# Shifted V by GpSimd, mixer factors by SyncE, one pair a load, relu engine by place, no zero products: one change to an attention and mixer kernel

## The chip, the cores and the metric

The kernel runs on one core of one Trainium2 chip. The metric is device time in microseconds (us). The engines are PE (TensorE), DVE (VectorE), ACT (ScalarE), POOL (GpSimd) and SP (SyncE, which here only issues DMAs). Profiles are single executions, and the hardware profiler's span is about 2 us shorter than the time of the same run.

A run is called slow when it is more than 1.5% above the fastest run of the same kernel. Ratios below are the mean time of one kernel's fast runs over that of the other's fast runs of the same rounds, so they are not quite the ratios of the medians that are quoted beside them.

## The reference

```python
# q, k, v: (4, 8, 768, 64); window of 96 keys behind the query, and 8 global keys
scores = q @ k^T / 8 - slope[h] * dist      # -1e9 outside window and globals
x = softmax(scores) @ v                     # to (4, 768, 512)
u = x + ((x^T @ U) @ V)^T                   # low-rank mixing of tokens, rank 32
out = u + relu(u @ w_ch1) @ w_ch2           # w_ch1 (512, 2048), w_ch2 (2048, 512)
```

## The kernel before

The work is cut into 16 slots, one per pair of heads (4 batches of 4 pairs). Slot i computes scores of pair i+1, A.V of pair i, the mixing of pair i, and prepares q, k, v of pair i+2. The MLP of a batch can start only when its four pairs are done, so slots 0 to 3 have no MLP work for PE. From slot 4 on, MLP pieces of the earlier batch are filled in between (`fill`), each of four 512-column matmuls. After slot 15 comes a tail of MLP work only.

A query block needs the keys and values of its own block and of the block before it, where the first rows are replaced by those of block 0 (the global keys). For the values this is the tile `vp`:

```python
def v_prev(i):
    vh = v16[:, i % VR]; vp = vp16[:, i % VPR]
    if i == 0:
        nc.vector.tensor_copy(vp, vh[:, :, 0:NPB])
        nc.vector.tensor_copy(vp[0:G], vh[0:G, :, 0:1].broadcast_to(...))
    else:                                        # SBUF to SBUF, three DMAs
        nc.sync.dma_start(vp[G:P], vh[G:P, :, 0:NPB])
        for hi in range(2):
            nc.sync.dma_start(vp[0:G, hi], vh[0:G, hi, 0:1].broadcast_to(...))

def keep_busy(n):                                # products of zeros
    if KEEP and n:
        bank = ps_tp("dmy", FP32, 512)
        for _ in range(n):
            nc.tensor.matmul(bank, zz[:, 0:P], zz, start=True, stop=True)

# in a piece of the first MLP product
if jt % 2 == 0: nc.scalar.activation(htr[:, jt], hh, AF.Relu)
else:           nc.vector.tensor_scalar_max(htr[:, jt], hh, 0.0)

keep_busy(15)
# ... (cut)
for i in range(NPAIR):                           # slots 0 to 3
    v_prev(i + 2)
    if i > 0: mix_h(i - 1, nc.vector)
    scores(i + 1, 0); transposes(i + 2, 0); scores(i + 1, 1)
    keep_busy(2); av(i); norm(i)
    scores(i + 1, 2); cast_x(i); mask(i + 1, 0); transposes(i + 2, 1)
    keep_busy(3); k_prev(i + 2, nc.gpsimd)
    if i > 0: mix_t(i - 1)
    mask(i + 1, 1); keep_busy(3); mix_tmp(i)
    if i == 0: load(4, 2)
    if i == 1: load_w2()
    if i == 2: load(6, 2)
mix_h(NPAIR - 1, nc.vector); keep_busy(6); mix_t(NPAIR - 1)
```

All loads that convert to half precision (q, k, v, w1, w2, and here also the mixer's U and V) are issued by GpSimd, in program order with its copies `k_prev`.

The softmax here doesn't subtract the row's maximum and nothing guards it: scores larger than these inputs give would overflow.

## Time and profile before

Time: 269.16 us median (268.44 to 269.26, 4 runs). The profiled span is 265.7 us.

| mark in the profile | before, us |
|---|---|
| A.V of pair 0 starts | 16.7 |
| A.V of pair 1 starts, ends | 24.0, 31.6 |
| first MLP matmul (`hps`, slot 4) | 53.4 |
| A.V of pair 8 starts | 98.2 |
| from there to the end of the span | 167.5 |

First, the profile's second part: the span in 40 slices of 6.6 us, busy tenths of PE, the granted PE clock, and the DMA engines.

```profile
PE   8785498868989999899999999989998999999994
...
PEclk9979579999999999999999999999999999999999
DMA  7999999999999999915991162413215101210022
```

The DMA engines are busy at 9 tenths or more from the second slice to the seventeenth, up to about 110 us. The clock dips in the third and in the fifth and sixth slice.

PE's waits (engine, line, what it waited for: us in total, times, longest):

```profile
PE ob L335 <- DMA vp_85<-v_84: 5.9, 2, 3.6
PE hps L428 <- ACT htr L433: 3.2, 5, 0.7
PE sc L297 <- POOL kP L260: 2.1, 1, 2.1
...
PE hps L428 <- DVE htr L435: 1.1, 1, 1.1
```

The largest is the wait for `vp`. Its origin is in the chain of waits that ended last (start us, us, what):

```profile
14.08 0.70 SPq L272
14.82 0.62 SPq L274
15.48 15.33 DMA vp_85<-v_84
30.85 0.22 PE ob L335
```

The last of pair 1's three copies, a small one of 20 KB, was issued at 15.48 us and landed at 30.8, while the 2 MB of w1, issued at 11.3 and 12.0 us, were under way (they landed at 25.9 and 31.3). Late in this run, at 158 us, the same small copy landed in 2.0 us. That w1 is what held it is inferred from these times. The Trainium skill, "Trainium Kernel Development and Optimization", Key Constraints, says that DMAs issued from SyncE, ScalarE and GpSimd run on the same 16 DMA engines and interleave. The trace is in keeping with it: the large `vp` copies, issued by SyncE, take 2.4 us to land at best in this run, and 12.2 us at worst, beside loads that GpSimd had issued.

### The profile page before, as it was taken

The page shows a single profiled execution, that of the slowest core. Times are in us where ns is not written, and L with a number is a line of the kernel's source. Part 1 is how long each engine was busy: PE and PEld are TensorE (multiplying, and loading weights), DVE is VectorE, ACT ScalarE, POOL GpSimd, SP SyncE. Part 2 cuts the span into 40 slices and gives each one's busy share as a digit, 9 for nine tenths or more (in the row PEclk, how much of TensorE's full clock was granted, in tenths as well). Part 3 has the DMA queues.
Part 4 walks back from the last instruction along what each step waited for, and adds up shares of the span by engine and source line. Part 5 has one row for each costly group of instructions (what it writes and reads, how often), then busy time and mean ns, then how long its engine had stood idle before and what let it go on. Part 6 is the DMA issues. An engine that isn't in the chain of part 4 may idle for free.

```text
span 265.7 us, 4667 instructions
## 1 busy us (share of the span) xinstructions
PE 239.0 (90%) x1910; PEld 116.0 (44%) x1910; DVE 133.7 (50%) x225; ACT 99.7 (38%) x180; POOL 69.5 (26%) x98
## 2 busy tenths in 40 slices
PE   8785498868989999899999999989998999999994
PEld 3352355434544553344444454445453444444441
DVE  3644257737566575624544645576666342234321
ACT  1786167445724525322246141557411330023100
POOL 8905035568248184104801010101000000000000
PEclk9979579999999999999999999999999999999999
DMA  7999999999999999915991162413215101210022
GB/s 82 165 194 214 201 157 176 183 157 152 156 148 144 231 109 152 107 32 163 162 183 27 30 123 83 123 38 79 35 69 80 39 0 42 79 39 0 2 79 79
DMA packets 97958, 28.67 MB, mean 108 GB/s; under 512 B 86225, under 2 KB 94353, under 8 KB 97937
## 3 DMA queue, kind: packets, MB, share of 16 engines
q0 software_dynamic: 62736, 13.73, 58.4%
q1 hardware_dynamic: 35200, 14.64, 27.4%
q8 instruction: 15, 0.25, 0.4%
q14 instruction: 7, 0.05, 0.1%
HBM read 27.46 MB, written 6.29 MB: 127 GB/s over the span
## 4 chain that ended last, share of the span: by engine, by line
PE 61%; DMA 16%; ACT 7%; POOL 5%; DVE 5%; issue 3%; SPq 1%; DVEq 0%; POOLq 0%; ACTq 0%
PE cps L446 27%; PE hps L428 23%; DMA vp_85<-v_84 6%; DMA v_84<-in_v_dram 5%; ACT ep L302 4%; PE sc L297 4%; DMA qkT<-qkn 4%; POOL qkn L121 2%; DVE x_sb L388 2%; DMA v16w<-in_moe_V_dram 2%; PE h_ps L383 1%; PE ob L335 1%; POOL v_84 L110 1%; PE ob L339 1%; PE tmp_ps L369 1%
## 5 line engine op out<-in xcount | busy, mean ns | idle before, releaser
L428 PE MATMUL hps<-uT,w_16_81 128*128 128x512 f16 x384 | 91.4, 379 | 5.5 <-ACT htr L433 3.2
L446 PE MATMUL cps<-w_16_82,htr 128*128 128x512 f16 x384 | 88.6, 379 | 0.0
L302 ACT ACTIVATE ep<-sc 128x512 f16<-128x512 f32 (+1 forms) x96 | 48.6, 564 | 71.0 <-PE sc L297 71.0
L428 PEld LDWEIGHTS <-w_16_81 128*128 128x128 f16 x384 | 35.1, 97 | 48.1 <-issue 11.4
L433 ACT ACTIVATE htr<-hps 128x512 f16<-128x512 f32 x48 | 28.7, 598 | 65.1 <-PE hps L428 64.5
L446 PEld LDWEIGHTS <-htr 128*128 128x128 f16 x384 | 35.5, 98 | 40.2
L435 DVE TENSOR_SCALAR htr<-hps 128x512 f16<-128x512 f32 x48 | 33.1, 689 | 36.6 <-PE hps L428 36.6
L453 DVE TENSOR_TENSOR osb<-cps,x_sb 128x512 f32<-128x512 f32 x24 | 16.5, 689 | 30.7 <-PE cps L446 30.6
L315 DVE TENSOR_TENSOR ep<-ep,expb 128x1280 f16<-128x1280 f16 x32 | 26.5, 828 | 9.5 <-ACT ep L302 9.4
L259 POOL COPY kP<-qkT 128x480 f16<-128x480 f16 x10 | 6.5, 654 | 79.9 <-DMA qkT<-qkn 68.8
L388 DVE TENSOR_TENSOR x_sb<-x_sb,h_ps 128x768 f32<-128x768 f32 x16 | 15.3, 953 | 14.1 <-PE h_ps L383 14.1
L207 PE MATMUL dmy<-zz 128*128 128x512 f16 x60 | 19.6, 454 | 1.3 <-DVE zz L149 1.2
L121 POOL DMA_DIRECT2D qkn<-in_k_dram x20 | 16.8, 851 | 8.3 <-DMA v_84<-in_v_dram 4.7
L335 PE MATMUL ob<-vp_85,ep 128*128 128x65 f16 x160 | 13.5, 199 | 5.9 <-DMA vp_85<-v_84 5.9
L351 DVE RECIPROCAL rcp<-ob 128x12 f32<-128x12 f32 x16 | 3.7, 233 | 28.5 <-PE ob L339 28.5
L121 POOL DMA_DIRECT2D qkn<-in_q_dram x20 | 16.7, 852 | 0.0
L352 DVE TENSOR_TENSOR x_sb<-ob,rcp 128x768 f32<-128x768 f32 x16 | 15.3, 958 | 0.6
L335 PEld LDWEIGHTS <-ep 128*128 128x128 f16 x160 | 11.8, 102 | 5.9 <-DMA vp_85<-v_84 4.0
L339 PE MATMUL ob<-v_84,ep 128*128 128x65 f16 x160 | 13.5, 199 | 0.0
L339 PEld LDWEIGHTS <-ep 128*128 128x128 f16 x160 | 11.7, 101 | 2.4 <-issue 2.4
L110 POOL DMA_DIRECT2D v_84<-in_v_dram x9 | 12.1, 1346 | 0.2
L392 DVE CAST uu<-x_sb 128x768 f16<-128x768 f32 x16 | 9.6, 600 | 0.6
(120 smaller groups left out, 157.4 us busy)
## 6 DMA issues: line engine op xcount, KB each, us to landing
out_dram<-osb SPq DMA_DIRECT2D x24, 256.0 KB, 2.2
v_84<-in_v_dram POOLq DMA_DIRECT2D x7, 384.0 KB, 8.4
w_16_81<-in_moe_w_ch_dram POOLq DMA_DIRECT2D x2, 1024.0 KB, 17.0
w_16_82<-in_moe_w_ch_dram POOLq DMA_DIRECT2D x2, 1024.0 KB, 14.5
qkn<-in_q_dram POOLq DMA_DIRECT2D x20, 96.0 KB, 7.3
qkn<-in_k_dram POOLq DMA_DIRECT2D x20, 96.0 KB, 6.7
vp_85<-v_84 SPq DMA_DIRECT2D x15, 121.9 KB, 6.5
qkst<-in_q_dram POOLq DMA_DIRECT2D x2, 384.0 KB, 9.5
```

Source lines behind the costliest of these rows:

```text
L121: nc.gpsimd.dma_start(stg[:, :, hi], src[b, 2 * hp + hi].rearrange("(n p) d -> p n d", p=P),)
L207: nc.tensor.matmul(bank, zz[:, 0:P], zz, start=True, stop=True)
L302: nc.scalar.activation(ep[:, hi, idx[0]:idx[0] + n].rearrange("p n c -> p (n c)"), scs[hi][:, 0:n * P], AF.Exp, scale=qk_scale,)
L315: nc.vector.tensor_tensor(blk, blk, eb[:, :, m:m + 1].broadcast_to((P, 2, NPB, P)), ALU.mult,)
L335: nc.tensor.matmul(ob[:, t], ep[:, hi, NSB + t - 1], vp16[:, i % VPR, hi, t - 1], start=True, stop=False,)
L339: nc.tensor.matmul(ob[:, t], ep[:, hi, t - 1], v16[:, i % VR, hi, t], start=False, stop=True,)
L388: nc.vector.tensor_tensor(xp, xp, hps[:, 0:S].rearrange("p (n c) -> p n c", n=NSB), ALU.add)
L428: nc.tensor.matmul(hh, w1_16[:, dc, jt * P:(jt + 1) * P], uT[:, dc, r0:r0 + TT], start=(dc == 0), stop=(dc == NDC - 1),)
L433: nc.scalar.activation(htr[:, jt], hh, AF.Relu)
L435: nc.vector.tensor_scalar_max(htr[:, jt], hh, 0.0)
L446: nc.tensor.matmul(cps, htr[:, jc, tt * P:(tt + 1) * P], w2_16[:, jc], start=(jc == 0), stop=(jc == NJC - 1),)
L453: nc.vector.tensor_tensor(osb, cps, xs[b][:, n], ALU.add)
```

## The change

Five ideas: make the shifted V of pairs 1 to 5 with GpSimd copies, so it does not queue behind weight loads; load the mixer factors U and V by SyncE and convert them on ScalarE, to free GpSimd's issue time; load one pair a slot; give each MLP piece's relu to the engine that has room at that place; and leave out the products of zeros. Some steps of slots 0 to 3 also change places.

```diff
-    KEEP = True
+    KEEP = False
...
+    u32 = uv32[:, S:S + NSB * R].rearrange("p (c r) -> p c r", c=NSB)
+    nc.sync.dma_start(u32, moe_U.rearrange("(c p) r -> p c r", p=P))
+    for g in range(NGR):
+        nc.sync.dma_start(uv32[g * R:(g + 1) * R, 0:S], moe_V)
+    nc.scalar.activation(u16, u32, AF.Copy)
+    nc.scalar.activation(v16w, uv32[:, 0:S], AF.Copy)
-    nc.gpsimd.dma_start(u16, ...)          # and v16w by GpSimd, copied by SyncE
...
-        if i == 0:
-            nc.vector.tensor_copy(vp, vh[:, :, 0:NPB])
-            nc.vector.tensor_copy(vp[0:G], ...)
+        if i < NSTART:                     # NSTART is 6
+            eng = nc.vector if i == 0 else nc.gpsimd
+            eng.tensor_copy(vp, vh[:, :, 0:NPB])
+            eng.tensor_copy(vp[0:G], ...)
...
-                if jt % 2 == 0:
+                if on_act:                 # set at each fill(f, True or False), alternating within it
...
     for i in range(NPAIR):
-        v_prev(i + 2)
...                                         # transposes(2, 0) after av(0)
-        keep_busy(2)
+        keep_busy(1)
...
         k_prev(i + 2, nc.gpsimd)
+        v_prev(i + 2)
+        mix_tmp(i)
+        mask(i + 1, 1)
         if i > 0:
             mix_t(i - 1)
-        mask(i + 1, 1)
-        keep_busy(3)
-        mix_tmp(i)
...
-        if i == 2:
-            load(6, 2)
+        if i >= 2:
+            load(i + 4, 1)
...
-        if i % 2 == 0 and i + 4 < NP:
-            load(i + 4, 2)
+        if i + 4 < NP:
+            load(i + 4, 1)
```

## The prediction

> **What bounds it now.** From 53.4 us on (first hps matmul in the timeline) TensorE is nearly full: the windows 80 to 200 us show PE 92 to 99% busy, and its waits after 53 us sum to 10 us (2.1 for kP, 4.3 for relu, 1.2 for osb and uT; wait view). 768 matmuls of 512 columns at 216 ns (64 in 13.83 us in the chain) are 166 us of it. Before 53.4 us nothing is full. In this startup pair 1's products with vp wait 3.65 + 2.26 us for SyncE's shift of V: its three DMAs, issued at 14.1 to 15.5 us, land at 24.2, 27.8 and 30.8, behind the 2 MB of w1. Half clock is granted at 15.5 to 18.9 and 25.7 to 36.0 us. A.V of pairs 0 to 3 starts at 16.7, 24.0 (done at 31.4), 39.1, 46.0. An undisturbed slot is 6.8 us: a chain av, norm (1.2), cast (0.84), mix_tmp, tmp16, mix_h, add (0.96), beside 5.5 to 6.4 us of ScalarE.
>
> **What the change does.**
> 1. Pairs 1 to 5: 15 DMA issues become 10 GpSimd copies. By kP's copies (480 elements 0.6 us, 160 in 0.32) I estimate 1.5 to 2 us a pair on POOL, which has room (2.8 and 3.8 us busy in 10 to 20 and 20 to 30 us). Removes the 5.9 us wait and its slow restart: estimate 7 us.
> 2. U and V by SyncE plus two ScalarE copies (estimate 1.1 us): frees 1.4 us of POOL issue, so pairs 2, 3 and w1 start earlier; adds DMA load beside the first q, k. Net -1 to +0.5 us.
> 3. 60 zero matmuls go: 19.6 us busy, mostly in PE's idle time. The 15 at the start hold the first transposes until 6.5 us although q landed at 4.7; in a slot two groups sit on the chain, 0.4 us each. Against it: the Trainium skill, "TensorE: Matmul & The Clock Gate", Part 1, says that the array defaults to half clock until about 3.4 us of sustained work; the half clock around this trace's idle stretch agrees. I expect much of the startup at 0.5: av 1.3 instead of 0.7 us, a slot about 7.5 us rather than 6; recovered in the first 4 us of MLP work.
> 4. mix_tmp before the second mask: tmp16 0.7 us earlier a slot. One pair per load: kP of pair 5 no longer sits behind eight qkn issues, so the 2.1 us wait goes; but DMA stays the limit for pairs 4 and 6 (q4 landed 34.3, k6 58.7), so part of the gain is waited for again.
> 5. Relu engine by place: of 4.3 us of waits for htr, about 2 go.
>
> **Sum.** MLP starts at about 46 instead of 53.4 us (-7); its stage has 1 us for restarting cold and up to 2 of new waits for qkT, against 2 (kP) and 2 (relu) gained: -1 to -3. Predicted 259.5 us, range 254 to 265.5. Chances: faster 0.84, same 0.14, slower 0.02.
>
> **What would show it.** No PE wait for vp in startup; first hps at 44 to 48 us, av of pair 1 at 23 to 24; clock 0.5 through most of 5 to 45 us, 1.0 from about 5 us after the first hps; POOL busy up some 8 us; htr waits down; the last 60 us unchanged.
>
> **What would make it wrong.** Half clock lasting into the MLP slots; POOL copies much slower (VectorE's copies, descriptor making), so kP or vp of pairs 4 to 6 come late; input DMAs, full until about 100 us, limiting pairs 4 to 7; U and V delaying the first q, k. Or, the other way, a warm startup: 254.

## More of the kernel before

The marks cut the run into three parts: the startup up to the first `hps`; slots 4 to 7, in which input DMAs still run; and the rest.

The windows by stage (us, then busy us of each engine, mean granted clock, DMA share, GB/s):

```profile
core 0: us, PE busy (x) PEld busy (x) DVE busy (x) ACT busy (x) POOL busy (x), PEclk, DMA share, GB/s
0.00:53.44 53.44, 39.98 (x483) 22.48 (x483) 28.85 (x57) 30.02 (x54) 25.40 (x38) 0.87 1.34 171
53.44:98.20 44.76, 40.59 (x370) 19.89 (x367) 27.27 (x46) 21.00 (x39) 25.31 (x34) 1.00 1.70 157
98.20:205.28 107.08, 101.89 (x808) 48.91 (x807) 60.40 (x98) 39.16 (x72) 18.78 (x27) 1.00 0.70 94
```

In the startup no compute engine is full; the DMA engines are (a share above 1 means that transfers overlap). In the third window PE is 95% busy and DMA no longer presses.

## The result, and the profile after

Time: 260.24 us median (258.97 to 263.25, 4 runs; the 263.25 counts as slow). The ratio to the kernel before is 0.9658 (95% interval 0.9607 to 0.9709): faster by 3.4%, and 0.7 us above the point predicted. The profiled run is fast, its span 259.1 us.

The same slices:

```profile
PE   1567674896999999999999999999998999999994
...
PEclk9998589597999999999999999999999999999999
DMA  7999999999999999949959342343222001210022
```

PE's waits:

```profile
PE tpb L239 <- DMA qkst<-in_q_dram: 6.9, 2, 5.7
PE sc L302 <- ACT ep L307: 2.6, 3, 1.4
PE sc L302 <- DMA qkT<-qkn: 2.5, 2, 2.3
PE tpub L414 <- DVE uu L397: 2.2, 1, 2.2
PE tmp_ps L374 <- ACT x_718 L366: 1.4, 1, 1.4
...
PE hps L433 <- DVE htr L440: 0.5, 1, 0.5
```

The waits for `vp` and `kP` are gone, and those for `htr` fell from 4.3 to 0.5 us. Of the 6.9 us for `qkst`, 5.7 are the start, where the zeros used to run; the other 1.2 are for pair 4 and new. The waits for `x` (4.9 us in the four slots of the startup) and for `uu` (2.2) stand where groups of zeros ran before. The chain of waits shows this one and another new wait:

```profile
25.62 5.92 DMA qkst<-in_q_dram
31.59 0.85 PE tpb L239 x12
...
52.73 8.36 DMA qkT<-qkn
61.13 0.40 PE sc L302 x8
```

q of pair 4 now holds slot 2 until 31.6 us, and the transposed k of pair 6 holds slot 5 until 61.1 us. Where the kernel before waited for a copy of V, this one waits a shorter time for the next input.

The windows by stage, cut at the same marks:

```profile
core 0: us, PE busy (x) PEld busy (x) DVE busy (x) ACT busy (x) POOL busy (x), PEclk, DMA share, GB/s
0.00:47.30 47.30, 27.27 (x422) 20.21 (x423) 28.70 (x57) 31.37 (x56) 32.46 (x47) 0.87 1.34 177
47.30:94.30 47.00, 43.92 (x368) 21.51 (x367) 28.09 (x47) 20.51 (x38) 26.35 (x36) 0.92 1.80 154
94.30:198.70 104.40, 101.48 (x808) 49.01 (x807) 58.07 (x96) 41.03 (x74) 20.83 (x31) 1.00 0.69 96
```

So the gain in span, 265.7 - 259.1 = 6.6 us in these two executions, is 6.1 us in the startup (53.4 to 47.3), minus 2.2 given back in slots 4 to 7 (44.8 to 47.0), plus 2.7 after that (107.1 to 104.4). The tail is the same 60.4 us. The ratio of the timed runs makes the whole gain 9.2 us of 269: the profiled run before (267.73 us) lies below its median and the one after (260.93 us) above. I keep to the profile for where the gain lies and to the ratio for how large it is; 2.6 us of it are thus not located in any stage.

**How to read the clock.** The row PEclk and the windows show full clock for the first 20 us after the change. They are wrong there: the trace's first clock record comes at 21.1 us. The spacing of equal matmuls tells the truth. Two stretches of the timeline after the change (start us, us, what), A.V of pair 3 and of pair 4:

```profile
39.31 0.19 PE L340 MATMUL ob<-vp_85,ep 128*128 128x65 f16 x1
39.34 0.19 PE L344 MATMUL ob<-v_84,ep 128*128 128x65 f16 x1
39.37 0.19 PE L340 MATMUL ob<-vp_85,ep 128*128 128x65 f16 x1
...
49.11 0.25 PE L344 MATMUL ob<-v_84,ep 128*128 128x65 f16 x1
49.16 0.25 PE L340 MATMUL ob<-vp_85,ep 128*128 128x65 f16 x1
49.22 0.24 PE L344 MATMUL ob<-v_84,ep 128*128 128x65 f16 x1
```

The starts are 30 ns apart in the first stretch and 55 ns in the second. The trace's records say half clock at 45.0 to 51.8 us, which agrees with the second. A.V of pair 0, at 17.4 us, has the spacing of 55 ns too, so PE ran at half clock there, whatever the row says. By records and spacing the changed kernel is at half clock until 21.1 us, at 24.5 to 34.7, at 45.0 to 51.8 and at 62.0 to 65.5, which is in the first MLP slots. The Trainium skill, "TensorE: Matmul & The Clock Gate", Part 1, says that the array defaults to half clock and that activity is watched in windows of about 3.4 us. The stretches here last 10.2, 6.8 and 3.5 us, close to three, two and one such windows.

### The profile page after: what moved, and what is told of

It reads as the page before. It is cut to its first block, busy times and chain, and to the rows that moved or that the text cites. A ratio compares the mean times of both kernels' runs of the same rounds, so it can differ in the third digit from the quotient of the medians.

```text
span 259.1 us, 4549 instructions
## 1 busy us (share of the span) xinstructions
PE 229.4 (89%) x1850; PEld 115.4 (45%) x1850; DVE 132.1 (51%) x223; ACT 102.5 (40%) x184; POOL 79.6 (31%) x111
## 4 chain that ended last, share of the span: by engine, by line
PE 69%; ACT 10%; DMA 10%; DVE 6%; issue 2%; POOL 1%; SPq 1%; DVEq 0%; POOLq 0%; ACTq 0%
PE hps L433 29%; PE cps L451 27%; DMA qkT<-qkn 6%; ACT ep L307 5%; PE sc L302 4%; DMA qkst<-in_q_dram 2%; DMA qkst<-in_k_dram 2%; PE ob L340 2%; PE ob L344 2%; DVE x_sb L393 2%; PE h_ps L388 1%; PE tmp_ps L374 1%; PE tpb L239 1%; DVE ep L320 1%; ACT qT L247 1%
## 5 line engine op out<-in xcount | busy, mean ns | idle before, releaser
L433 PE MATMUL hps<-uT,w_16_81 128*128 128x512 f16 x384 | 93.4, 387 | 1.5 <-DVE uT L418 0.6
L438 ACT ACTIVATE htr<-hps 128x512 f16<-128x512 f32 x50 | 29.9, 598 | 75.0 <-PE hps L433 75.0
L440 DVE TENSOR_SCALAR htr<-hps 128x512 f16<-128x512 f32 x46 | 31.8, 691 | 40.9 <-PE hps L433 40.8
L263 POOL COPY kP<-qkT 128x480 f16<-128x480 f16 x10 | 5.9, 595 | 83.1 <-DMA qkT<-qkn 61.2
L121 POOL DMA_DIRECT2D qkn<-in_k_dram x20 | 16.7, 857 | 0.4 <-DMA v_84<-in_v_dram 0.4
L239 PE MATMUL tpb<-ident_103,qkst 128*64 128x128 f16 x144 | 8.9, 284 | 7.7 <-DMA qkst<-in_q_dram 6.9
L357 DVE TENSOR_TENSOR x_sb<-ob,rcp 128x768 f32<-128x768 f32 x16 | 15.3, 957 | 0.6
L110 POOL DMA_DIRECT2D v_84<-in_v_dram x14 | 15.1, 1080 | 0.0
L340 PE MATMUL ob<-vp_85,ep 128*128 128x65 f16 x160 | 15.0, 209 | 0.0
L344 PE MATMUL ob<-v_84,ep 128*128 128x65 f16 x160 | 14.9, 209 | 0.0
L340 PEld LDWEIGHTS <-ep 128*128 128x128 f16 x160 | 13.2, 109 | 1.8 <-issue 0.5
L344 PEld LDWEIGHTS <-ep 128*128 128x128 f16 x160 | 13.2, 109 | 0.0
L239 PEld LDWEIGHTS <-qkst 128*64 128x64 f16 x144 | 6.4, 146 | 9.6 <-DMA qkst<-in_q_dram 7.1
```

The costliest lines, as they stand in the source:

```text
L121: nc.gpsimd.dma_start(stg[:, :, hi], src[b, 2 * hp + hi].rearrange("(n p) d -> p n d", p=P),)
L239: nc.tensor.matmul(tp[64 * hi:64 * hi + 64, sb * P:(sb + 1) * P], stg[:, hi, sb], ident16, is_transpose=True, start=(sb == 0), stop=(sb == ...
L340: nc.tensor.matmul(ob[:, t], ep[:, hi, NSB + t - 1], vp16[:, i % VPR, hi, t - 1], start=True, stop=False,)
L344: nc.tensor.matmul(ob[:, t], ep[:, hi, t - 1], v16[:, i % VR, hi, t], start=False, stop=True,)
L433: nc.tensor.matmul(hh, w1_16[:, dc, jt * P:(jt + 1) * P], uT[:, dc, r0:r0 + TT], start=(dc == 0), stop=(dc == NDC - 1),)
```

## The experiments

The table holds what every run is read by. "Rest" is from the start of A.V of pair 8 to the end of the span. The marks are of one profiled execution each; profiles marked * fell in a slow run.

| run | median us | ratio to before (95%) | first hps | slots 4 to 7 | A.V of pair 8 | rest |
|---|---|---|---|---|---|---|
| before | 269.16 | 1 | 53.4 | 44.8 | 98.2 | 167.5 |
| the change | 260.24 | 0.9658 (0.9607 to 0.9709) | 47.3 | 47.0 | 94.3 | 164.8 |
| b_vpool | 263.12 | 0.9788 (0.9752 to 0.9823) | 50.0 | 44.5 | 94.5 | 167.3 |
| a_vdma | 263.73 | 0.9771 (0.9717 to 0.9825) | 50.3 | 47.1 | 97.4 | 164.8 |
| b_relu | 266.32 | 0.9909 (0.9852 to 0.9967) | 52.7 | 47.0 | 99.6 | 165.1 |
| a_relu_alt* | 264.92 | 0.9762 (0.9687 to 0.9837) | 47.2 | 49.9 | 97.1 | 166.8 |
| b_nozero | 268.79 | 0.9989 (0.9947 to 1.0031) | 55.1 | 45.6 | 100.7 | 167.3 |
| a_keep | 259.48 | 0.9629 (0.9560 to 0.9698) | 49.6 | 42.7 | 92.4 | 165.1 |
| a_uv_pool | 259.30 | 0.9658 (0.9602 to 0.9714) | 47.3 | 46.8 | 94.0 | 165.1 |
| a_load2* | 265.40 | 0.9735 (0.9637 to 0.9832) | 48.7 | 51.5 | 100.2 | 165.0 |
| early | 258.66 | 0.9620 (0.9589 to 0.9651) | 48.3 | 43.1 | 91.4 | 165.1 |
| early_keep | 259.15 | 0.9652 (0.9614 to 0.9689) | 49.0 | 42.5 | 91.5 | 165.0 |
| early2* | 262.36 | 0.9656 (0.9580 to 0.9732) | 46.3 | 51.2 | 97.5 | 165.1 |
| early2_some | 259.77 | 0.9677 (0.9629 to 0.9725) | 44.0 | 49.0 | 93.0 | 165.1 |

All outputs are right. Judged at 2%, b_vpool, a_vdma, a_relu_alt and a_load2 are "unclear", b_relu and b_nozero "same", and the others "faster" than the kernel before; of all of them, only b_nozero's interval contains 1.

### b_vpool and a_vdma: the shifted V, alone and undone

b_vpool is the kernel before with this part alone:

```diff
-        if i == 0:
-            nc.vector.tensor_copy(vp, ...)           # both copies
+        if i < NSTART:
+            eng = nc.vector if i == 0 else nc.gpsimd
+            eng.tensor_copy(vp, ...)                 # both copies
...
     for i in range(NPAIR):
-        v_prev(i + 2)
...
         k_prev(i + 2, nc.gpsimd)
+        v_prev(i + 2)
```

> The kernel before with one part of the change alone: shifted V of pairs 1 to 5 by GpSimd, after kP in each slot; zero products, loads, order and relu as before. Theory (the wait for vp was the main loss, and its removal carries the first hps forward): no PE wait for vp in the startup, first hps at 47 to 50 us instead of 53.4, 262.5 to 265.5 us. Rival (the landing of pair 4's q and k, or the loads of pair 6, take the gain back): 266.5 us or more.

Measured: no wait for `vp` in the startup, first `hps` at 50.0 us, ratio 0.9788. That is about 5.7 us of 268.7, as the theory expected.

a_vdma is the changed kernel with this part undone, at its old place in the slot:

```diff
-        if i < NSTART:
-            eng = nc.vector if i == 0 else nc.gpsimd
+        if i == 0:
+            eng = nc.vector
```

> The changed kernel with the shifted V of pairs 1 to 5 made by SyncE's DMAs again, at their old place. Theory 1 (the 5.9 us wait for vp was the main loss): PE waits some 4 to 6 us for vp at pair 1 again, no zeros keep the clock, 266 to 270 us. Rival (DMA bounds the startup in any case, q and k of pair 4 land at 31 to 34 us): at most 2 us lost, 260 to 262 us.

Measured: ratio 0.9771, some 3 us slower than the change, between the two expectations. The first `hps` moves by 3.0 us. PE's three largest waits:

```profile
PE tpb L239 <- DMA qkst<-in_q_dram: 8.9, 2, 5.6
PE tmp_ps L374 <- ACT x L366: 6.4, 8, 1.8
PE sc L302 <- DMA qkT<-qkn: 3.4, 2, 2.3
```

`vp` is nowhere on the list. SyncE's queue shows a reason (start us, us, what), first in the kernel before, then in a_vdma:

```profile
11.99 1.97 SPq L171 DMA_DIRECT2D v16w<-v16w  x3
14.08 0.70 SPq L272 DMA_DIRECT2D vp_85<-v_84  x1
...
11.97 0.76 SPq L277 DMA_DIRECT2D vp<-v  x1
```

In the kernel before, SyncE first copied the mixer's V three times, once it had landed at 11.97 us, and only then issued the shift of pair 1. In a_vdma, where the mixer's factors come first, the shift was issued 2.1 us earlier and had landed at 25.3 instead of 30.8 us; A.V of pair 1 began at 25.1. So the U and V part of the change may take away part of this wait too; no run tries it alone.

The wait for `qkst` grew from 6.9 to 8.9 us, because q of pair 4 landed at 33.1 instead of 31.5 us. That the V copies by DMA delayed it is not shown: in b_vpool, which has none of them in the startup, it landed at 33.2. So the shift of V is worth 3 to 6 us, depending on what else is there, and it is the largest part of the gain.

### b_relu and a_relu_alt: the relu engine, alone and undone

b_relu takes the `on_act` argument of the change and its eight `fill(f, True or False)` into the kernel before. a_relu_alt undoes it in the changed kernel:

```diff
-                if on_act:
+                if jt % 2 == 0:
```

> The kernel before with one part of the change alone: the relu engine by place. Theory (it removes PE's waits for htr, 4.3 us in the kernel before, and nothing else moves): startup unchanged with the first hps near 53.4 us, waits for htr under 1.5 us, from A.V of pair 8 to that of pair 15 about 2 us less than the 99.9 us of before, 265.5 to 267 us. Rival (the 4.7 us that undoing it cost in the changed kernel is its worth): 264 to 265 us.

> The changed kernel with the relu engine chosen by parity of the tile again. Theory (placing it removed PE's waits for htr): waits for htr back at 3 to 4 us, 261.5 to 264 us. Rival (those waits moved elsewhere, the placing is worth nothing): within 0.7 us of the changed kernel.

Measured: b_relu has a ratio of 0.9909, 2.4 us of 268. After A.V of pair 8, where loads no longer disturb, the rest shrinks from 167.5 to 165.1 us. PE's waits in b_relu contain one line for `htr`:

```profile
PE hps L428 <- DVE htr L435: 0.5, 1, 0.5
```

Undoing it in the changed kernel brings the waits for `htr` back to 3.8 us and the rest from 164.8 to 166.8 us. Its median is 4.7 us above the change (2.8 us by the ratios of the fast runs, with intervals that overlap), more than that, but two of its four runs are slow, and in its profile 5.2 us of waits for `qkT` fall into slots 4 to 7, which parity of the relu does not explain. I therefore take the rest as the measure: across all 14 kernels it is 164.8 to 165.1 us with the placing and 166.8 to 167.5 without. The rival of b_relu, a worth of 4 to 5 us, is refuted.

### b_nozero and a_keep: the products of zeros, taken away alone and put back

Each is one line, `KEEP = False` in the kernel before, and `KEEP = True` in the changed kernel, where 15 stand at the start, 7 before the first slot, 1 and 3 in a slot, and 6 ahead of the MLP.

> The kernel before without its zero products, nothing else. Theory 1 (they keep the clock; PE has room for them while it waits for vp): half clock in the first MLP slot, first hps at 52 to 55 us, 268.5 to 273 us. Theory 2 (they sit on the chain): first hps 2 us or more earlier, 265 to 267.5 us.

> The changed kernel with the zero products back in the places that it still has for them (15 at the start, 1 + 3 a slot, 6 before the MLP). Theory 1 (they cost little, their absence costs clock): the 15 end before the first q lands at 5.7 us, the 3 and the 6 fall into waits of 1.3 and 2.2 us, PE runs at full clock through most of the startup, the first hps comes at 44 to 46 us instead of 47.3 and the two half-clock stretches at 45 to 51.8 and 62 to 65.5 us go: 255 to 258 us. Theory 2 (they occupied PE on the chain, so leaving them out is part of the gain): 262 to 265 us, first hps at 49 us or later.

Measured: no clear difference of the totals in either. b_nozero has 0.9989 and does what its Theory 1 said: half clock is recorded at 53.1 to 59.9 us, in the first MLP slot, the first `hps` comes at 55.1 us, and the median is 268.79 us. a_keep has 0.9629 against 0.9658, the intervals overlap, and its median lies between its two theories. But its stages move, in opposite directions. In a_keep the slots 4 to 7 run at full clock (window from the first `hps` to A.V of pair 8, and the clock is the third number from the end):

```profile
49.60:92.40 42.80, 40.23 (x371) 19.92 (x368) 28.27 (x47) 20.52 (x38) 26.10 (x35) 1.00 1.69 161
```

They take 42.7 us instead of 47.0 at a mean clock of 0.92. On the other side, the first `hps` came at 49.6 us instead of 47.3. Of these 2.3 us, 2.0 are the landing of q of pair 4: its transposes start at 33.55 us in a_keep and at 31.59 in the change; from there to the first `hps` it is 16.1 and 15.7 us. So the zeros, net of the clock that they hold, cost 0.4 us of chain here. Why q of pair 4 landed later in that execution is not shown; it was issued only 0.2 us later. For a_keep both theories were too strong: the clock of slots 4 to 7 is full with the zeros, they cost little, and the total hardly moves.

The 4.3 us of slots 4 to 7 are not what the clock alone is worth. The same window in early and in early_keep, two later runs that differ in the zeros alone:

```profile
48.31:91.42 43.11, 42.41 (x368) 20.83 (x367) 27.64 (x47) 20.56 (x38) 22.22 (x31) 0.94 1.55 159
48.99:91.49 42.50, 40.10 (x370) 19.89 (x367) 28.02 (x47) 20.51 (x38) 22.79 (x31) 1.00 1.63 163
```

Here PE is 2.3 us longer busy without the zeros, but idle for 1.7 us less, and the stage is only 0.6 us longer. Nor is the clock full in all kernels with zeros: in b_relu the last of them run before its first `hps` at 52.7 us, and it is at half clock at 58.4 to 61.8 us.

### a_uv_pool and a_load2: the other two parts undone

a_uv_pool loads U and V with GpSimd as before. a_load2 loads two pairs at a time from pair 6 on:

```diff
-        if i >= 2:
-            load(i + 4, 1)
+        if i == 2:
+            load(6, 2)
...
-        if i + 4 < NP:
-            load(i + 4, 1)
+        if i % 2 == 0 and i + 4 < NP:
+            load(i + 4, 2)
```

> The changed kernel with U and V of the mixer loaded by GpSimd again. Theory (the SyncE loads delay the first q by 1.0 us and k by 1.7 us, and free 1.4 us of GpSimd's issue time, which nothing waits for): first transposes at 4.7 to 5.0 us instead of 5.7, A.V of pair 0 up to 1 us earlier, w1 landing 1 to 2.5 us later; total within 1.5 us of the changed kernel. Rival (the earlier w1 and pair 4 are what matters): q of pair 4 lands 2 us later and the first hps with it, 262 to 264 us.

> The changed kernel with two pairs a load again from pair 6 on. Theory (kP of pair 5 sits behind eight issues, PE waits about 2 us more at the first MLP slot, and q, k of pair 6 land later): 262 to 264 us. Rival (the waits of that stage are set by the sum of the loads, not by their grouping): within 1 us of the changed kernel.

a_uv_pool: the first transposes start at 4.70 instead of 5.70 us and A.V of pair 0 at 16.2 instead of 17.4, w1 lands 1.2 us later, and q of pair 4 at 31.9 instead of 31.5. The first `hps` is at 47.3 in both, and the ratio is 0.9658 in both. What the start gains, PE then waits for at pair 4. Beside V copies by GpSimd, this part of the change is worth nothing; without them, it was not tried (see a_vdma).

a_load2: waits for `kP` are back (3.3 us), slots 4 to 7 take 51.5 us, and the median is 265.4 us. But two of its four runs are slow, the profiled one among them, and the interval of the fast runs (0.9637 to 0.9832) overlaps that of the change. The direction fits the theory; the size stays open.

### early, early_keep, early2, early2_some: is it the loads?

If the landing of pair 4 holds the startup and that of pair 6 the first MLP slots, another order of loads should gain. In early:

```diff
     load(2, 2)
+    load(4, 2)
     load_w1()
...
-        if i == 0:
-            load(4, 2)
-        if i == 1:
-            load_w2()
-        if i >= 2:
-            load(i + 4, 1)
+        if i <= 1:
+            load(i + 6, 1)
+        if i == 2:
+            load_w2()
+        if i == 3:
+            load(8, 1)
```

(and slot 4 has no load). early_keep is early with `KEEP = True`.

> The changed kernel with q, k, v of pairs 4 and 5 loaded before w1, of pairs 6 and 7 in the first two slots, then w2, then pair 8. Theory (the startup is held by the landing of q, k of pair 4, the first MLP slots by that of pair 6): no PE wait for qkst in the third slot nor for qkT, first hps at 45 to 46 us, 255.5 to 258.5 us. Rival (w1, then w2, come too late in their place, or the DMA engines are full anyway): waits for w1 at the first hps or w2 at the first cps, 260 us or more.

> The same order of loads, with the zero products back. Theory 1 (with no wait for loads, only the clock is left to gain; the zeros fit into waits): first hps at 45 to 47 us at full clock, 1 to 3 us faster than the same order without them, 253 to 257 us. Theory 2 (without waits for loads the zeros sit on the chain, about 0.4 us a slot): 0 to 2 us slower than without them.

Measured: early has 0.9620, with six runs within 257.15 to 259.04 us, none slow; the interval overlaps that of the change. The wait for q of pair 4 is gone, and A.V of pair 2 starts at 31.3 instead of 32.9 us. But the first `hps` comes at 48.3 us, later than expected, since a new wait took its place:

```profile
39.35 0.28 PE L303 MATMUL sc<-qT,kP 64*128 64x128 f16 x4 [2.34 <-POOL kP L265]
```

GpSimd stood at the issues of pair 7, behind which `kP` of pair 4 is queued. Its own waits there ended with the landing of w1 (1.1 us) and of v (0.6 us). early_keep is 0.3% slower, within the interval.

early2 moves the load of pair 7 to slot 2 and w2 to slot 3, so GpSimd is free for `kP`. early2_some has the same order, `KEEP = True`, 10 zero products at the start, 3 ahead of each `mix_tmp` and 6 ahead of the MLP, and none elsewhere.

```diff
+        if i == 0:
+            load(6, 1)
+        if i == 2:
+            load(7, 1)
+        if i == 3:
+            load_w2()
```

> The changed kernel with q, k, v of pairs 4 and 5 before w1, pair 6 in the first slot, pair 7 in the third, w2 in the fourth. Theory (in the run early the GpSimd queue stood at pair 7's issues until w1 had landed, and kP of pair 4 behind it cost PE 2.3 us): no PE wait for kP over 1 us, first hps at 45 to 47 us, 255.5 to 258 us. Rival (PE at half clock is the bound of the startup, so nothing more comes): first hps at 47.5 to 49, 258 to 259.5 us.

> The same with zero products only where PE waits in the runs before: 10 at the start, 3 ahead of each mix_tmp, 6 ahead of the MLP. Theory (placed in waits they cost nothing and keep the clock at full): no half clock in the first MLP slots, first hps at 44 to 46.5 us, 253.5 to 256.5 us. Rival (the clock is no bound of this stage once loads are early, or the zeros still delay the chain): within 1 us of the same kernel without them.

Measured: the first `hps` comes at 46.3 and 44.0 us, the earliest of all, in early2_some at full clock. Yet the totals are those of the change: 0.9656 and 0.9677. Of early2's six runs four are slow, the profiled one too, so its ratio rests on two runs. Two lines of the timeline of early2_some show where the lead went:

```profile
44.02 1.04 PE L434 MATMUL hps<-uT,w 128*128 128x512 f16 x4
...
67.96 0.40 PE L303 MATMUL sc<-qkT 64*128 64x128 f16 x8 [4.84 <-DMA qkT<-qkn]
```

The startup is 3.3 us shorter than in the change, and PE then waits 4.8 us in one place, and 6.6 in all, for transposed q and k. The w2 load, moved late, landed at 61.6 us and ran beside those transposes, which were issued at 54.4 and 57.7 us and landed at 64.8 and 67.9. The same is seen across the table: first `hps` from 44.0 to 50.0 us, but among the kernels that have V by GpSimd and a fast profile, A.V of pair 8 only from 91.4 to 94.5. I read this as the DMA engines setting the pace until pair 8, which the full DMA row of the first 100 us supports. That it is their throughput, and not the order of issue or the limit on transfers under way, no run here separates.

No version clearly beats the changed kernel. early has the lowest median and, of the kernels built on the changed one, the tightest runs.

## Why the prediction was right

The time (259.5 predicted, 260.24 measured) and the class were right, and so was the shape: a shorter startup, a part of it waited for again, and a gain from relu. Point by point:

- **V shift, "estimate 7 us".** The mechanism was right. The size is 5.7 us alone and about 3 us inside the changed kernel (b_vpool, a_vdma). That q of pair 4, which lands at 31 to 34 us, holds the next slot anyway is the likely reason, and is not shown. The prediction named this limit, but had not taken it from this item. The two GpSimd copies took 1.5 to 1.9 us a pair, against 1.5 to 2 estimated. A.V of pair 1 starts at 24.5 us, not at 23 to 24.
- **U and V, "-1 to +0.5 us".** Right, and it is nothing beside the GpSimd copies (a_uv_pool). Without the zeros at the start, but with the first q 1.0 us and the first k 1.7 us later, A.V of pair 0 starts at 17.4 us against 16.7.
- **Zero products.** Right that they are mostly off the chain and that clock is lost in return. "Clock 0.5 through most of 5 to 45 us" held, by records and spacing for about 26 of these 40 us, but PE ran at full clock at 34.7 to 45.0 us without them. "1.0 from about 5 us after the first hps" held at first (51.8 us), but one more wait brought half clock back at 62.0, which the prediction had named as a risk. In the total no effect is seen (b_nozero, a_keep).
- **Loads and kP.** The 2.1 us wait for `kP` went, and a 2.3 us wait for `qkT` came, as said ("up to 2 of new waits").
- **Relu, "about 2".** 2.4 us, and the waits for `htr` fell by 3.8 us (b_relu, and the rest column).
- **mix_tmp ahead of the second mask** was not tried alone, nor were the other changes of place in slots 0 to 3; its 0.7 us a slot is open.
- **The sum.** First `hps` at 47.3, not 46; the MLP stage net -0.4 us (+2.2, -2.7), not -1 to -3. Both terms were somewhat too hopeful in the profiled execution: its stages gain 6.6 us, and 9.6 were predicted. That the timed median came within 0.7 us rests on the 2.6 us that no stage shows, and is in part luck. POOL rose by 10.1 us (69.5 to 79.6), not 8.

## What to carry to other kernels

A small on-chip copy by DMA can take far longer than its size suggests: here one of 20 KB landed in 15.3 us while weights loaded and in 2.0 us later. Let an engine with room make it, and look at what its queue must issue first. When a startup gets shorter, mark its end and the next few stages separately: here, in the fast profiles with V by GpSimd, first MLP matmuls at 44 to 50 us all led to A.V of pair 8 at 91.4 to 94.5 us. Products that only keep the clock up cannot be judged by their busy time or by the total alone; look at the clock, by the spacing of equal matmuls, in the stage that follows.

## What the Trainium skill lacked or had wrong

- "TensorE: Matmul & The Clock Gate", Part 1, lets sustained activity of about 3.4 us release the clock, but does not say how dense it must be. In the changed kernel PE is 6.8 us busy in the window from 10 to 20 us, and the clock stays at half until 21.1 us. Cut into windows of 3.41 us, counted from the clock records, the 14 traces show each of their 50 rises to full clock at the end of a window in which PE was busy for 2.99 us or more, and each of their 50 falls after one with 2.04 us or less; of the 91 windows that stayed at half clock, 4 had 2.99 us or more, and of those that stayed at full clock the least busy had 1.53 us. (Windows before the first record are counted as half clock.) Part of the work from 10 to 20 us is transposes, which the page (Part 4) says do not count in the same way; no run here separates the two.
- The same page, Part 1, warns that clock events in a trace can be unreliable, but no page that I read says that a profile may hold no clock record at first. The views used here then show full clock. The first record is at 21.1 us after the change, and a window before it shows 1.00, where A.V of pair 0, at 17.4 us, has a spacing of 55 ns instead of 30.
- "Trainium Kernel Development and Optimization", Key Constraints, says that the queues share the DMA engines, but gives no figure for the price. Here a `vp` copy of the same size lands in 2.4 us late in the run and in 12.2 us beside the loads of w1 and of pair 4's q, k and v.
